# Linear attention on one Trainium2 core: from six tiles of 120 columns to five of 128, with a reordered start

## The chip, the cores and the metric

The kernel runs on one core of one Trainium2 chip. Time is device microseconds (us) for one execution, lower is better. Engines are named as in the profile: PE is the TensorE matmul engine, PEld its weight loads (they overlap the matmuls: 122.3 us of them beside 244.4 us of PE in the 275.5 us of the kernel before), DVE is VectorE, ACT is ScalarE, POOL is GpSimd, SP is SyncE, which here only issues DMAs. "q" after an engine's name means its instruction queue. The profile traces one execution; its span (first to last instruction) is about 1.7 us shorter than the device time of the same execution (275.5 for 277.27 us before).

## The reference

Two linear-attention blocks A and B read the same input x of 2048 rows and 640 columns; a sigmoid gate mixes their results. There are 32 heads of 20 columns. All data is bf16.

```python
def attn(x, wqkv, wo):                       # x (1, 2048, 640); H = 32, Dh = 20
    q, k, v = split_heads(x @ wqkv)          # wqkv (640, 1920)
    phi = lambda t: where(t > 0, t + 1, exp(t)) + 1e-6
    pq, pk = phi(q), phi(k)
    kv  = einsum("bhsd,bhse->bhde", pk, v)   # 20 x 20 per head
    z   = einsum("bhsd->bhd", pk)
    num = einsum("bhqd,bhde->bhqe", pq, kv)
    den = einsum("bhqd,bhd->bhq", pq, z)[..., None] + 1e-6
    return merge_heads(num / den) @ wo
g   = sigmoid((x * gate_w).sum(-1))
out = g * attn(x, A_wqkv, A_wo) + (1 - g) * attn(x, B_wqkv, B_wo)
```

The kernel uses phi(t) = min(exp(t), 1) + max(t, 0) + 1e-6: an exponential on ACT and two DVE operations. The per-head products become 128-row matmuls by putting several heads in one tile and masking the result to the heads' diagonal squares.

## The kernel before

It has a start (loads and constants), four projection blocks of 512 rows, and an output stage. The 640 columns are cut into six tiles: five of 120 columns (6 heads) and one of 40. No head crosses a tile edge, so one matmul per tile gives the numerator. Cut to what matters (`p` is the path, A or B):

```python
# start, inside block 0
load_weights_act()      # SP: gwt, 1.2 KB, the gate vector
load_weights_sync()     # SP: wq
load_weights_pool()     # POOL: wkv of A, then wo of A and B
build_consts()          # POOL: masks, and E4, which spreads a head's scale over its columns
nc.vector.tensor_copy(out=gw32[:], in_=gwt[...])     # L171: the gate as a matmul operand
load_weights_sync2()    # SP: wkv of B
...
for tb in range(4):                                  # projection block of 512 rows
    gps = ...           # 5 matmuls: the gate sums (L176)
    for p in range(2):
        for b in range(6):                           # q tile
            # 5 matmuls -> qps (L191); ACT: qe = exp (L194)
            # DVE: qr = max(qps,0)+1e-6 (L196); pqT = min(qe,1)+qr (L198)
    for tti in range(4):                             # 128 rows of keys and values
        for ct in range(5):                          # 512 of A k, A v, B k, B v
            # 5 matmuls -> kps (L212)
            for (r0, r1, kind, p) in regions:        # in column order
                # key part: exp on ACT, two DVE operations -> pk_st
                # value part: ACT copies into windows of 120 plus a column of ones -> vz
        # 6 matmuls per path: kvps += pk_st x vz (L248)
# DVE: KVbd = kvps * mask, Zm (z spread over heads)
...
def stage_A(tb):        # denominators dps; numerators nps, copied to nb by ACT
    for b in range(6):
        nc.tensor.matmul(nps, lhsT=KVbd[p][:, b, :], rhs=pqT[p][:, b, rows], start=True, stop=True)
def stage_B(tb):        # rps = E4 x (gate/denominator); DVE: oT = nb * rps, 12 per block
def stage_C(tb):        # output projection
    for tti in range(4):
        ops = pso.tile([P, 640], F32)                # pso has one buffer
        # 2 paths x 6 tiles x (512 and 128 columns) = 24 matmuls (L324)
        nc.scalar.copy(out=ob, in_=ops)              # L331
```

## Time and profile before

| Before | |
|---|---|
| Device time, median of 16 runs | 277.29 us (275.94 to 278.33) |
| Profiled span | 275.5 us |
| Start, until the first gate matmul | 18.2 us |
| Projection blocks, until the first numerator matmul | 161.7 us |
| Output stage | 95.6 us |

The profile's page begins with each engine's busy time and share of the span.

```profile
span 275.5 us, 4403 instructions
...
PE 244.4 (89%) x1668; PEld 122.3 (44%) x1668; DVE 163.9 (59%) x345; ACT 134.3 (49%) x429; POOL 16.4 (6%) x40
```

PE is busy 89% of the span. That alone does not say how near it is to its limit, because the records of matmuls overlap: one 512-column matmul is recorded at 379 ns, but 22 of them (`kps L212 x22` in the chain below) take 4.76 us, 216 ns each. I count matmuls at this spacing.

The chain that ended last, in order of time (start us, length us, engine or DMA, what, line):

```profile
3.81 13.52 DMA gwt<-in_gate_w_dram
17.36 0.83 DVE gw L171
18.23 2.31 PE gps L176 x5
...
47.43 4.76 PE kps L212 x22
...
64.67 1.20 DVE qr L196 x2
65.87 1.20 DVE pqT L198 x2
```

PE does nothing until 18.23 us, because a 1.2 KB load of the gate vector takes 13.5 us to land. Its five first matmuls take 2.31 us, about 0.42 us apart, so PE starts slowly. Below, PE is called cold while 512-column matmuls come about 0.42 us apart, and warm when they come 0.216 us apart. Later the chain runs through DVE's pairs, 1.20 us for two q tiles in each of two operations, so 1.20 us per q tile, where PE needs 5 x 0.216 = 1.08 us.

PE's timeline, first gate matmul of each projection block and the first numerator:

```profile
18.23 2.31 PE L176 MATMUL gps<-xT,gw 128*128 128x512 bf16 x5 [18.23 <-DVE gw L171]
...
58.67 0.38 PE L176 MATMUL gps<-xT,gw 128*128 128x512 bf16 x1
...
98.64 0.38 PE L176 MATMUL gps<-xT,gw 128*128 128x512 bf16 x1
...
138.60 0.38 PE L176 MATMUL gps<-xT,gw 128*128 128x512 bf16 x1
...
179.91 0.85 PE L295 MATMUL nps<-pqT,KVbd 128*128 128x512 bf16 x3
```

The blocks repeat every 39.97 us (58.67 to 98.64, 98.64 to 138.60).

ACT's timeline, copies of finished output tiles (last field: idle before, and who ended it):

```profile
241.37 0.69 ACT L331 CAST ob<-ops 128x640 bf16<-128x640 f32 x1 [7.33 <-issue]
245.62 0.69 ACT L331 CAST ob<-ops 128x640 bf16<-128x640 f32 x1 [3.55 <-PE ops L324]
249.86 0.69 ACT L331 CAST ob<-ops 128x640 bf16<-128x640 f32 x1 [3.55 <-PE ops L324]
```

These come 4.24 us apart. There is one ops buffer, so each period is 24 matmuls and their drain (3.42 us in PE's timeline, 225.12 to 228.54), the copy (0.69 us), and only then the next tile (229.36).

### The profile page before, as it was taken

The page shows a single profiled execution, that of the slowest core. Times are in us where ns is not written, and L with a number is a line of the kernel's source. Part 1 is how long each engine was busy: PE and PEld are TensorE (multiplying, and loading weights), DVE is VectorE, ACT ScalarE, POOL GpSimd, SP SyncE. Part 2 cuts the span into 40 slices and gives each one's busy share as a digit, 9 for nine tenths or more (in the row PEclk, how much of TensorE's full clock was granted, in tenths as well). Part 3 has the DMA queues.
Part 4 walks back from the last instruction along what each step waited for, and adds up shares of the span by engine and source line. Part 5 has one row for each costly group of instructions (what it writes and reads, how often), then busy time and mean ns, then how long its engine had stood idle before and what let it go on. Part 6 is the DMA issues. An engine that isn't in the chain of part 4 may idle for free.

```text
span 275.5 us, 4403 instructions
## 1 busy us (share of the span) xinstructions
PE 244.4 (89%) x1668; PEld 122.3 (44%) x1668; DVE 163.9 (59%) x345; ACT 134.3 (49%) x429; POOL 16.4 (6%) x40
## 2 busy tenths in 40 slices
PE   0039999999999999999999999989999999988874
PEld 0014444444444444444444444434556545555442
DVE  2016995558985639985549976569942922932400
ACT  3006565665555575466674565699651444022121
POOL 8950000000000000000000000000000000000000
PEclk9999999999999999999999999999999999999999
DMA  7999500031000000000000000000010010010101
GB/s 187 340 325 289 130 4 0 1 63 34 0 0 2 1 0 2 0 0 1 2 1 0 0 2 0 0 2 4 1 45 28 26 48 26 24 50 24 48 26 48
DMA packets 17492, 12.30 MB, mean 45 GB/s; under 512 B 12148, under 2 KB 16758, under 8 KB 17472
## 3 DMA queue, kind: packets, MB, share of 16 engines
q1 hardware_dynamic: 16608, 8.52, 11.6%
q0 software_dynamic: 864, 3.50, 3.7%
q8 instruction: 13, 0.21, 0.3%
q14 instruction: 7, 0.06, 0.1%
HBM read 6.66 MB, written 2.62 MB: 34 GB/s over the span
## 4 chain that ended last, share of the span: by engine, by line
PE 52%; DVE 21%; ACT 15%; DMA 5%; issue 5%; SPq 1%; ACTq 0%; DVEq 0%
PE kps L212 20%; PE ops L324 18%; DVE qr L196 8%; DVE pqT L198 7%; PE qps L191 5%; DMA gwt<-in_gate_w_dram 5%; ACT vz L238 4%; ACT nb L297 4%; PE kvps L248 4%; ACT ob L331 3%; DVE r_st L225 3%; PE rps L310 2%; PE gps L176 2%; DVE pk_st L227 2%; PE nps L295 2%
## 5 line engine op out<-in xcount | busy, mean ns | idle before, releaser
L212 PE MATMUL kps<-wkv,xT 128*128 128x512 bf16 x400 | 94.5, 379 | 0.5
L324 PE MATMUL ops<-woh,oT 128*128 128x512 bf16 (+1 forms) x384 | 60.1, 299 | 4.6 <-ACT ob L331 4.1
L212 PEld LDWEIGHTS <-xT 128*128 128x128 bf16 x400 | 38.1, 97 | 41.2 <-issue 2.4
L191 PE MATMUL qps<-xT,wq 128*128 128x512 bf16 x240 | 53.5, 383 | 0.0
L312 DVE TENSOR_TENSOR oT<-nb,rps 128x512 bf16<-128x512 bf16 x48 | 30.9, 686 | 30.4 <-PE rps L310 22.3
L238 ACT CAST vz<-kps 128x120 bf16<-128x120 f32 (+4 forms) x224 | 35.8, 260 | 18.7 <-PE kps L212 14.9
L225 DVE TENSOR_SCALAR r_st<-kps 128x512 bf16<-128x512 f32 (+1 forms) x64 | 30.5, 486 | 21.6 <-ACT e_st L223 21.6
L324 PEld LDWEIGHTS <-oT 128*128 128x128 bf16 x384 | 30.2, 98 | 25.6 <-issue 5.5
L194 ACT ACTIVATE qe<-qps 128x512 bf16<-128x512 f32 x48 | 28.3, 597 | 21.9 <-DVE pqT L198 12.0
L196 DVE TENSOR_SCALAR qr<-qps 128x512 bf16<-128x512 f32 x48 | 31.1, 682 | 13.3 <-ACT qe L194 13.3
L223 ACT ACTIVATE e_st<-kps 128x512 bf16<-128x512 f32 (+1 forms) x64 | 27.7, 463 | 19.5 <-PE kps L212 19.5
L191 PEld LDWEIGHTS <-wq 128*128 128x128 bf16 x240 | 23.7, 99 | 29.6 <-issue 2.2
L331 ACT CAST ob<-ops 128x640 bf16<-128x640 f32 x16 | 11.1, 692 | 49.0 <-PE ops L324 37.4
L198 DVE SCALAR_TENSOR_TENSOR pqT<-qe,qr 128x512 bf16<-128x512 bf16 x48 | 31.1, 682 | 0.2
L227 DVE SCALAR_TENSOR_TENSOR pk_st<-e_st,r_st 128x512 bf16<-128x512 bf16 (+1 forms) x64 | 30.1, 488 | 1.2
L297 ACT CAST nb<-nps 128x512 bf16<-128x512 f32 x48 | 25.3, 643 | 8.0 <-PE nps L295 7.5
L176 PE MATMUL gps<-xT,gw 128*128 128x512 bf16 x20 | 7.2, 440 | 18.2 <-DVE gw L171 18.2
L248 PE MATMUL kvps<-vz,pk_st 128*128 128x121 bf16 (+1 forms) x192 | 20.1, 212 | 2.3 <-ACT vz L238 1.7
L248 PEld LDWEIGHTS <-pk_st 128*128 128x128 bf16 x192 | 13.9, 97 | 15.8 <-DVE pk_st L227 6.8
L310 PEld LDWEIGHTS <-E 128*128 128x128 bf16 x192 | 13.9, 97 | 9.0 <-issue 4.2
L310 PE MATMUL rps<-rgT,E 128*128 128x128 bf16 x192 | 17.5, 218 | 0.3
L295 PE MATMUL nps<-pqT,KVbd 128*128 128x512 bf16 x48 | 16.2, 380 | 1.4 <-ACT nb L297 0.2
(46 smaller groups left out, 62.7 us busy)
## 6 DMA issues: line engine op xcount, KB each, us to landing
out_dram<-ob SPq DMA_DIRECT2D x16, 160.0 KB, 1.8
wkv<-in_A_wqkv_dram POOLq DMA_DIRECT2D x2, 800.0 KB, 8.2
wkv<-in_B_wqkv_dram SPq DMA_DIRECT2D x2, 800.0 KB, 10.8
woh<-in_A_wo_dram POOLq DMA_DIRECT2D x1, 800.0 KB, 9.3
woh<-in_B_wo_dram POOLq DMA_DIRECT2D x1, 800.0 KB, 9.2
wq<-in_B_wqkv_dram SPq DMA_DIRECT2D x1, 800.0 KB, 13.2
wq<-in_A_wqkv_dram SPq DMA_DIRECT2D x1, 640.0 KB, 14.4
wq<-in_A_wqkv_dram SPq DMA_DIRECT2D x1, 160.0 KB, 13.2
```

What stands on the lines that cost most here:

```text
L191: nc.tensor.matmul(qps[:, :], lhsT=wq[p][:, fo, BOFF[b]:BOFF[b] + P], rhs=xT[:, fo, :], start=(fo == 0), stop=(fo == NFO - 1))
L196: nc.vector.tensor_scalar(out=r[:], in0=qps[:, :], scalar1=0.0, scalar2=1e-6, op0=ALU.max, op1=ALU.add)
L198: nc.vector.scalar_tensor_tensor(out=pqT[p][:, b, tb * TB:(tb + 1) * TB], in0=e[:], scalar=1.0, in1=r[:], op0=ALU.min, op1=ALU.add)
L212: nc.tensor.matmul(kps[:, :], lhsT=xT[:, fo, tti * TT:(tti + 1) * TT], rhs=wkv[:, fo, ct * 512:(ct + 1) * 512], start=(fo == 0), stop=(fo ...
L225: nc.vector.tensor_scalar(out=r_st[:, d0:d0 + n], in0=kps[:, a0 - c0:a1 - c0], scalar1=0.0, scalar2=1e-6, op0=ALU.max, op1=ALU.add)
L227: nc.vector.scalar_tensor_tensor(out=pk_st[:, d0:d0 + n], in0=e_st[:, d0:d0 + n], scalar=1.0, in1=r_st[:, d0:d0 + n], op0=ALU.min, op1=ALU ...
L238: nc.scalar.copy(out=vz_st[:, d0:d0 + n], in_=kps[:, c - c0:c - c0 + n])
L248: nc.tensor.matmul(kt[:msz, off:off + bs + 1], lhsT=pk_st[:, p * D + BOFF[b]:p * D + BOFF[b] + msz], rhs=vz_st[:, p * VZW + WIN * b:p * VZ ...
L297: nc.scalar.copy(out=nb[:], in_=nps[:, :])
L310: nc.tensor.matmul(rps[:, j * TT:(j + 1) * TT], lhsT=E4[j][:, BOFF[b]:BOFF[b] + P], rhs=rgT[:, 0:TT], start=True, stop=True)
L312: nc.vector.tensor_tensor(out=oT[p][:, b, :], in0=nsbs[b][:], in1=rps[:, :], op=ALU.mult)
L324: nc.tensor.matmul(ops[:, j0:j1], lhsT=oT[p][:, b, tti * TT:(tti + 1) * TT], rhs=woh[p][:, b, j0:j1], start=(i == 0), stop=(i == 2 * NBLK ...
```

## The change

The intent is to use all 128 rows: 640 = 5 x 128, so one tile in six goes away in q, in the key-value products and in the output projection. The price is that heads straddle tile edges. A numerator tile needs small corner products from its neighbours: 13 matmuls per path instead of 6 in blocks 0 and 1. For blocks 2 and 3 the corner rows are gathered by small DMAs into one extra operand, which makes it 10. Four other things change with it: POOL builds constants before it issues weight loads and issues wo last; ten dummy matmuls run in the idle start; mask products are made by 13 small matmuls; and value copies come before key work within a projection tile. The gate vector keeps its place: it is still SP's first load after x. With the layout itself the value copies on ACT become wider and fewer (128 instead of 224), and a memset in each projection tile goes away. The diff is cut to what matters.

```diff
-NBLK = 6
-BROWS = [120, 120, 120, 120, 120, 40]
+NB = 5
+PAIRS = {}           # for tile m: the tiles b whose heads reach into it; 13 pairs in all
+CORNER = []          # the rows of a neighbour that tile m needs
...
             if tb == 0:
-                load_weights_act()
                 load_weights_sync()
+                build_consts()
                 load_weights_pool()
-                build_consts()
+                build_e4()
+                load_wo()
+                for i in range(10):
+                    nc.tensor.matmul(wps[:, :], lhsT=KVbd[0][:, 4, :], rhs=KVbd[0][:, 0:4, :],
+                                     start=True, stop=True)
+                for m in range(NB):
+                    for b in PAIRS[m]:
+                        nc.tensor.matmul(mps[:, 0:P], lhsT=Hind[b][:, :], rhs=Hind[m][:, :], ...)
+                        nc.scalar.copy(out=masks[:, PIDX[(b, m)], :], in_=mps[:, 0:P])
...
+            if tb == NTB - 1:
+                for p in range(2):
+                    for (b, m, r0, r1, o) in CORNER:
+                        nc.sync.dma_start(out=pqc[p][o:o + r1 - r0, :], in_=pqT[p][r0:r1, b, 2 * TB:4 * TB])
...
-                    for (r0, r1, kind, p) in regions:
+                    for (r0, r1, kind, p) in sorted(regions, key=lambda r: r[2] == "k"):
...
-                nc.tensor.matmul(nps[:, :], lhsT=KVbd[p][:, b, :], rhs=rq, start=True, stop=True)
+                if tb >= 2:
+                    nc.tensor.matmul(nps[:, :], lhsT=KVbd[p][:, PIDX[(m, m)], :], rhs=pqT[p][:, m, rows], ...)
+                    nc.tensor.matmul(nps[:, :], lhsT=KVc[p][0:NCR, m, :], rhs=pqc[p][0:NCR, ...], ...)
+                    bl = []
+                for i, b in enumerate(bl):
+                    nc.tensor.matmul(nps[:, :], lhsT=KVbd[p][:, PIDX[(b, m)], :], rhs=rq, ...)
...
-                    for b in range(NBLK):     # output projection: 24 matmuls per tile
+                    for m in range(NB):       # 20
```

## The prediction

> **What bounds the kernel now.** PE, in three stages (timeline and chain of waits).
> (1) Start, 0–18.2 us: PE waits for gw, a copy of gwt; the chain shows gwt's 1.2 KB load taking 13.5 us to land, issued at 3.8 us while the POOL queue moves 3.5 MB of weights. The first projection matmuls then start 425 ns apart, later ones 216 ns (22 in 4.76 us): a cold start of about 9 matmuls, 1.8 us.
> (2) Projections, 18.2–179.9 us: four blocks with a period of 40.0 us. PE work per block is 165 matmuls x 0.216 = 35.6 us plus 48 small kvps matmuls, about 2.3 us; the other 2 us are waits, mostly in the q part, where DVE needs 1.2 us per q tile (chain: pairs of 1.20 us) and PE only 1.08.
> (3) Output, 179.9–272.4 us: 16 output tiles, mostly 4.24 us apart: 24 matmuls (3.26 us), drain, the 0.69 us ACT copy of ob, next tile. The single ops buffer forbids overlap; three blocks' first tiles are longer (DVE's oT products, 0.62 us each).
>
> **The change.** 640 columns in five full 128-row tiles instead of six of 120. Heads straddle tiles, so the numerator needs corner products: 13 matmuls per path and block instead of 6 in blocks 0–1; in blocks 2–3, 10 (corners gathered by small DMAs). POOL builds constants before it issues weight loads, and PE gets 10 dummy matmuls and 13 mask matmuls in the idle start.
>
> **Costs.**
> - Start: without POOL's traffic ahead, the input transpose (5.0 us to landing when alone, DMA view) should be followed by gwt at about 7.5–8 us, gw at 9.[...] First projection matmul at about 9.5 us: −9. The dummy matmuls should keep PE warm[...]: −1.5. Then perhaps a wait for wq: +1.
> - Projections: per block 10 q matmuls fewer (−2.16 us; −2.4 where DVE paces), kvps 40 of 141–161 columns for 48 of 121/41 (about +0.2): −2.15 x 4 = −8.6.
> - Output: numerator matmuls 48 → 92, +9.5 us of PE; ops 384 → 320, −8.7; rps −1.8. PE's sum hardly moves, the latency chain does: tile 4.24 → 3.65 us (20 matmuls), 12 undisturbed tiles, −7. Block starts: 10 oT products for 12, partly refilled with numerator matmuls, −2.5. The first numerators (52 matmuls, PE-bound, where ACT's 24 copies were the limit) delay the first oT: +1.5. Together −8.
>
> 277.1 − 9 − 1.5 + 1 − 8.6 − 8 = 251.0. **Predicted 251 us, 8 in 10 between 244.5 and 257.** Faster by over 2%: 0.97; within 2%: 0.02; slower: 0.01.
>
> **What would show it.** First gps matmul near 9.5 us at 216 ns spacing; block period 37.8 us; output stage about 84.5 us with undisturbed tiles 3.6–3.7 us apart; DVE q pairs still 1.20 us in the chain; nb copies no longer back to back after the first numerators.
>
> **What would make it wrong.** gwt still slow by itself (640 two-byte pieces), or wq/wkv late, so that the start gains only 4 us; PE going cold again before gps; the 20 corner and mask products on DVE delaying the first numerators; numerator matmuls not fitting the gaps between output tiles, so that stage 3 becomes PE-bound and gains only 4 us.

The −9 rests on the trace of the kernel before, where gwt is late beside POOL's loads. That the dummies would keep PE warm (−1.5) was my estimate, out of the 1.8 us that the cold start costs in that trace; no run had yet shown it.

## The result

| | Before | After |
|---|---|---|
| Device time, median | 277.29 us (16 runs) | 250.00 us (8 runs, 249.53 to 250.03) |
| Profiled span | 275.5 us | 248.2 us |
| Start | 18.2 us | 8.2 us |
| Projection blocks | 161.7 us | 149.6 us |
| Output stage | 95.6 us | 90.4 us |

The ratio is 0.9015, 95% interval 0.8998 to 0.9032. Ratios in this document are the mean time of one kernel's runs over that of the other's runs of the same rounds, so they are not quite the ratio of the medians quoted. Executions over 1.5% slower than the fastest of the same kernel are left out of the means.

The same views of the kernel after. First the page's engine shares:

```profile
span 248.2 us, 4126 instructions
...
PE 235.6 (95%) x1535; PEld 117.7 (47%) x1535; DVE 152.3 (61%) x336; ACT 121.4 (49%) x326; POOL 26.1 (11%) x76
```

The chain that ended last, in order of time:

```profile
1.86 4.36 PE wps L213 x10
...
6.63 1.57 PE mps L218 x9
8.20 1.21 PE gps L225 x5
...
14.54 1.20 DVE pqT L247 x2
15.73 1.20 DVE qr L245 x2
```

The gate vector's load is off the chain: dummies (wps) and mask products (mps) fill PE until 8.2 us. The five gate matmuls take 1.21 us instead of 2.31. DVE's pairs still take 1.20 us each, now for ten q tiles per block.

PE's timeline, first gate matmul of each block and the first numerator:

```profile
8.16 1.24 PE L225 MATMUL gps<-xT,gw 128*128 128x512 bf16 x5
...
45.11 0.38 PE L225 MATMUL gps<-xT,gw 128*128 128x512 bf16 x1
...
82.38 0.38 PE L225 MATMUL gps<-xT,gw 128*128 128x512 bf16 x1
...
119.64 0.38 PE L225 MATMUL gps<-xT,gw 128*128 128x512 bf16 x1
...
157.77 6.21 PE L381 MATMUL nps<-pqT,KVbd 128*128 128x512 bf16 x28
```

The block period is 37.26 us (82.38 to 119.64), 2.71 less than before.

ACT's timeline, output copies:

```profile
218.24 0.69 ACT L418 CAST ob<-ops 128x640 bf16<-128x640 f32 x1 [6.54 <-issue]
221.94 0.69 ACT L418 CAST ob<-ops 128x640 bf16<-128x640 f32 x1 [3.01 <-PE ops L411]
225.64 0.69 ACT L418 CAST ob<-ops 128x640 bf16<-128x640 f32 x1 [3.01 <-PE ops L411]
```

The tile period is 3.70 us, 0.54 less.

The start gained 10.1 us, the projections 12.1 and the output stage 5.2. The forecast had 9, 9.1 (8.6 and 1.5 less a feared wait of 1) and 8. So the total was nearly exact while its parts were not, and the parts needed experiments.

### The profile page after: what moved, and what is told of

It reads as the page before. It is cut to its first block, busy times and chain, and to the rows that moved or that the text cites. A ratio compares the mean times of both kernels' runs of the same rounds, so it can differ in the third digit from the quotient of the medians.

```text
span 248.2 us, 4126 instructions
## 1 busy us (share of the span) xinstructions
PE 235.6 (95%) x1535; PEld 117.7 (47%) x1535; DVE 152.3 (61%) x336; ACT 121.4 (49%) x326; POOL 26.1 (11%) x76
## 4 chain that ended last, share of the span: by engine, by line
PE 63%; DVE 24%; ACT 7%; issue 4%; ACTq 0%; DVEq 0%
PE kps L265 26%; PE ops L411 17%; DVE qr L245 10%; DVE pqT L247 9%; PE nps L381 5%; PE kvps L302 5%; ACT ob L418 3%; DVE pk_st L280 2%; PE rps L397 2%; DVE r_st L278 2%; PE gps L225 2%; PE nps L376 2%; PE wps L213 2%; PE nps L374 2%; ACT th L229 2%
## 5 line engine op out<-in xcount | busy, mean ns | idle before, releaser
L411 PE MATMUL ops<-woh,oT 128*128 128x512 bf16 (+1 forms) x320 | 50.6, 299 | 4.2 <-ACT ob L418 4.0
L293 ACT CAST vz<-kps 128x240 bf16<-128x240 f32 (+6 forms) x128 | 31.4, 299 | 26.8 <-PE kps L265 26.8
L399 DVE TENSOR_TENSOR oT<-nb,rps 128x512 bf16<-128x512 bf16 x40 | 25.7, 686 | 30.3 <-PE rps L397 30.1
L240 PE MATMUL qps<-xT,wq 128*128 128x512 bf16 x200 | 43.8, 379 | 0.0
L411 PEld LDWEIGHTS <-oT 128*128 128x128 bf16 x320 | 25.4, 98 | 24.4 <-issue 6.4
L245 DVE TENSOR_SCALAR qr<-qps 128x512 bf16<-128x512 f32 x40 | 25.9, 681 | 14.7 <-ACT qe L243 14.7
L243 ACT ACTIVATE qe<-qps 128x512 bf16<-128x512 f32 x40 | 23.4, 597 | 16.5 <-DVE pqT L247 12.6
L247 DVE SCALAR_TENSOR_TENSOR pqT<-qe,qr 128x512 bf16<-128x512 bf16 x40 | 26.0, 681 | 0.1
L302 PE MATMUL kvps<-vz,pk_st 128*128 128x141 bf16 (+1 forms) x160 | 20.3, 228 | 0.9 <-DVE pk_st L280 0.5
L381 PE MATMUL nps<-pqT,KVbd 128*128 128x512 bf16 x52 | 12.1, 380 | 0.0
```

The lines of the kernel that those rows point to most:

```text
L240: nc.tensor.matmul(qps[:, :], lhsT=wq[p][:, fo, P * b:P * b + P], rhs=xT[:, fo, :], start=(fo == 0), stop=(fo == NFO - 1))
L245: nc.vector.tensor_scalar(out=r[:], in0=qps[:, :], scalar1=0.0, scalar2=1e-6, op0=ALU.max, op1=ALU.add)
L247: nc.vector.scalar_tensor_tensor(out=pqT[p][:, b, tb * TB:(tb + 1) * TB], in0=e[:], scalar=1.0, in1=r[:], op0=ALU.min, op1=ALU.add)
L293: nc.scalar.copy(out=vz_st[:, d0:d0 + n], in_=kps[:, c - c0:c - c0 + n])
L302: nc.tensor.matmul(kt[:, off:off + WW[b]], lhsT=pk_st[:, p * D + P * b:p * D + P * b + P], rhs=vz_st[:, p * VZW + WST[b]:p * VZW + WEN[b]] ...
L399: nc.vector.tensor_tensor(out=oT[p][:, m, :], in0=nsbs[m][:], in1=rps[:, :], op=ALU.mult)
```

## The experiments

Names that begin with b are edits of the kernel before, those with a edits of the kernel after. Every run gave correct results, and each kernel has four timed executions, made in turn with the kernel before on the same chip. They were made in four calls; the kernel before had medians of 277.39, 276.66, 277.53 and 277.30 us in them, so medians of different calls can differ by up to 0.9 us for no other reason. The kernel after (250.0 us) was not run again. Its ratio, 0.8998 to 0.9032, is the safer comparison: of the edits of the kernel after, only a_no_dummies has an interval that overlaps it.

| Run | Median us | Ratio to before | Against 250.0 |
|---|---|---|---|
| b_consts_first | 267.02 | 0.9627 (0.9603 to 0.9651) | |
| a_weights_first | 260.31 | 0.9388 (0.9360 to 0.9416) | +10.3 |
| a_no_dummies | 250.81 | 0.9045 (0.9024 to 0.9066) | +0.8 |
| a_k_first | 251.82 | 0.9076 (0.9053 to 0.9099) | +1.8 |
| b_all_but_layout | 264.55 | 0.9544 (0.9503 to 0.9585) | +14.6 |
| a_no_gather | 252.57 | 0.9113 (0.9073 to 0.9153) | +2.6 |
| a_split_ops | 246.78 | 0.8910 (0.8878 to 0.8942) | −3.2 |
| a_q_relu_act | 247.23 | 0.8925 (0.8891 to 0.8958) | −2.8 |
| a_gather1 | 248.56 | 0.8952 (0.8926 to 0.8978) | −1.4 |
| a_split_qrelu | 244.24 | 0.8796 (0.8770 to 0.8821) | −5.8 |
| a_all_three | 243.12 | 0.8753 (0.8723 to 0.8783) | −6.9 |
| a_wo_early | 253.62 | 0.9153 (0.9088 to 0.9219) | +3.6 |

### The start: is POOL's weight traffic what delays the gate vector?

My theory was that the 1.2 KB load is slow because POOL's megabytes use the same DMA engines. The rival was that it is slow by itself (640 pieces of two bytes; the trace of the kernel before has 640 DMA packets of this size), or that other edits moved the start. Two runs move only the order, one in each kernel.

```diff
 # b_consts_first (kernel before)
-                load_weights_pool()
                 build_consts()
+                load_weights_pool()
 # a_weights_first (kernel after)
+                load_weights_pool()
+                load_wo()
                 build_consts()
-                load_weights_pool()
                 build_e4()
-                load_wo()
```

> The kernel before with one thing moved: POOL builds its constants before it issues its weight loads. Theory (gate vector delayed by POOL's weight traffic on the shared DMA engines): gwt lands by about 7 us instead of 17.3, first gate matmul at about 8 us still cold (425 ns apart), time 277.1 - 10 = about 267 us. Rival (gwt is slow by its own 640 two-byte pieces, or the new kernel's start came from its other edits): gwt still lands after 15 us, time stays near 277 us.

> The kernel after with POOL's weight loads (wkv and wo) moved back ahead of the constants, the dummies kept. Theory: gwt lands near 17 us again, the first gate matmul starts at 17 to 18 us[...], time 250 + 10 to 12 = 260 to 262 us. Rival: unchanged within 2 us.

The chains of b_consts_first and of a_weights_first, the gate vector's load:

```profile
3.53 3.06 DMA gwt<-in_gate_w_dram
```

```profile
3.84 11.83 DMA gwt<-in_gate_w_dram
```

PE's timelines of the same two, the first gate matmuls:

```profile
7.50 2.32 PE L176 MATMUL gps<-xT,gw 128*128 128x512 bf16 x5 [7.50 <-DVE gw L171]
```

```profile
16.57 2.31 PE L225 MATMUL gps<-xT,gw 128*128 128x512 bf16 x5 [5.39 <-DVE gw L221]
```

With POOL quiet, the same load lands in 3.1 us; with POOL's loads ahead it takes 11.8 us. Moving the order alone gives 10.3 us in the kernel before (277.3 to 267.0) and takes 10.3 us away in the kernel after. (That the two agree to a tenth is chance: in the second, the start is only 8.4 us later, 16.57 against 8.16, and most of the rest is a PE that has gone cold again: from the first gate matmul to the first key-value matmul it takes 13.79 us, 16.57 to 30.36, against 11.86 in the kernel after.) The theory stands, and the rival falls. In the kernel before, between 10 and 12 us, the times of the 142 packets of POOL's queue (0.72 MB) add up to 103% of the time of the 16 DMA engines, and those of the 144 packets of gwt's queue, all of two bytes, to 4.2%. So the two queues share the engines; in what order an engine takes their packets is not shown.

In a_weights_first PE went cold again: the gate matmuls take 2.31 us although dummies and mask matmuls had run before. The granted clock on this run's page, in slices of 6.45 us, is 0.9 or more in the first, 0.7 in the second, 0.5 in the third (12.9 to 19.35 us, with the gate matmuls in it) and 0.9 or more again from the fourth on. If it fell once, from 1.00 to 0.50, that was between 9.0 and 10.3 us, an estimate from the second slice's 0.7. Then the 5.39 us of idleness before the gate matmuls (the bracket in their line) did not bring the fall, because these begin at 11.2 us. A single mask product at 10.87 us already took 0.31 us, where those at 8.26 and 8.89 us took 0.22. What makes the clock fall or rise is not shown. Nor does the granted clock show every cold PE: in the kernel before it reads 1.00 from 14 to 20 us, over five gate matmuls with the same 2.31 us. The cold state has to be read from the spacing.

### The dummies

```diff
-                wps = ps1.tile([P, 512], F32, name="wps", tag="ps1")
-                for i in range(10):
-                    nc.tensor.matmul(wps[:, :], lhsT=KVbd[0][:, 4, :], rhs=KVbd[0][:, 0:4, :], ...)
```

> The kernel after without the 10 dummy matmuls; the 13 mask matmuls stay. Theory (dummies are what warms PE): the first 8 or so projection matmuls run 425 ns apart, PE's q part ends about 1.7 us later, but DVE paces that part at 1.20 us per tile against PE's 1.08, so only part of it survives: time 250.0 + 0.8 to 1.8 us. Rival (dummies do nothing, or the mask matmuls alone keep it warm): within 0.3 us of 250.0.

PE's timeline of a_no_dummies:

```profile
7.84 2.32 PE L221 MATMUL gps<-xT,gw 128*128 128x512 bf16 x5 [0.92 <-DVE gw L217]
...
46.63 0.81 PE L221 MATMUL gps<-xT,gw 128*128 128x512 bf16 x3
```

The five gate matmuls take 2.32 us instead of 1.24, so the dummies do warm PE, though they multiply operands just set to zero and are themselves cold (ten in 4.36 us in the kernel after, 0.43 us apart); the 13 mask matmuls alone do not. The last group of gate matmuls of the second block comes 38.79 us after the first gate matmul, against 37.69 in the kernel after (8.16 to 45.85): 1.1 us longer. The start is 0.3 us earlier, which leaves the 0.8 us of the medians. The intervals of the ratios overlap slightly, so it is the trace that carries this, not the times. I had counted 1.5 us, and PE's slow start does cost about that: from the first gate matmul to the first key-value matmul it takes 13.30 us (7.84 to 21.14) against 11.86 (8.16 to 20.02), 1.44 longer. About 0.3 us is won back in the first projection tile, where PE has to wait less for DVE (25 matmuls in 5.56 us instead of 5.88), and 0.3 by the earlier start.

### Value copies before key work

The block period fell by 2.71 us where I had forecast 2.15. The forecast had overlooked one line of the diff, the sort of the regions.

```diff
-                    for (r0, r1, kind, p) in sorted(regions, key=lambda r: r[2] == "k"):
+                    for (r0, r1, kind, p) in regions:
```

> The kernel after with the order of the projection tile's copies put back: key part before value part. The block period fell by 2.71 us where 2.15 was forecast; theory A says the value-first order gave the missing half microsecond: block period 37.8 us instead of 37.26, time about 252.2. Theory B says it is the missing memset, wider copies and fewer kvps matmuls: block period stays within 0.15 us of 37.26 and the time within 0.6 us of 250.0.

PE's timeline of a_k_first, the first gate matmuls of the third and fourth block, and the key-value product that follows the first of them:

```profile
82.96 0.38 PE L225 MATMUL gps<-xT,gw 128*128 128x512 bf16 x1
83.69 0.28 PE L302 MATMUL kvps<-vz,pk_st 128*128 128x141 bf16 x2 [0.36 <-ACT vz L293]
...
120.60 0.59 PE L225 MATMUL gps<-xT,gw 128*128 128x512 bf16 x2
```

The period is 37.64 us, 0.38 longer, and the time is 1.8 us longer, where theory A had said 37.8 and 252.2. Theory A holds for most of the missing 0.56 us. The trace also shows where the time goes. At a block's border PE's five gate matmuls are woven with the last key-value products of the block before, and these wait for ACT's last value copies (the 0.36 us in the second line above). From the first gate matmul to the first q matmul it takes 1.70 us in this run (82.96 to 84.66) and 1.39 in the kernel after (82.38 to 83.77), so 0.31 of the 0.38 us lies there. In the view of waits, PE's key-value products waited for ACT's value copies 8 times, 1.7 us in all, in the kernel before, twice, 0.7 us, in this run, and never in the kernel after.

### Is the rest the layout, and do the parts add?

The kernel before received three of the side edits, POOL's constants before its weights, the dummies and the sort. It kept its early wo and its six tiles.

```diff
-                load_weights_pool()
                 build_consts()
+                load_weights_pool()
...
                 load_weights_sync2()
+                wps = ps1.tile([P, 512], F32, name="wps", tag="ps1")
+                for i in range(10):
+                    nc.tensor.matmul(wps[:, :], lhsT=KVbd[0][:, 4, :], rhs=KVbd[0][:, 0:4, :], ...)
...
-                    for (r0, r1, kind, p) in regions:
+                    for (r0, r1, kind, p) in sorted(regions, key=lambda r: r[2] == "k"):
```

> The kernel before with the change's three side edits (POOL's constants before its weights, the 10 dummy matmuls, value copies before key copies) but its own six tiles of 120 rows. Sum theory (the parts simply add): 277.3 - 10.3 - 0.8 - 1.8 = 264.4 us, so that the layout itself is worth the remaining 14.4 us. Rival (the layout's share is larger or smaller because the parts overlap): more than 1.5 us away from 264.4.

PE's timeline of b_all_but_layout:

```profile
27.01 2.33 PE L216 MATMUL kps<-wkv,xT 128*128 128x512 bf16 x10 [1.08 <-DMA wkv<-in_B_wqkv_dram]
...
87.63 0.59 PE L180 MATMUL gps<-xT,gw 128*128 128x512 bf16 x2
...
127.04 0.59 PE L180 MATMUL gps<-xT,gw 128*128 128x512 bf16 x2
```

It measured 264.55 us, so the parts add. That they do so within 0.2 us is partly luck. The sort is worth 0.56 us per block here (39.97 to 39.41), 2.2 in all and not 1.8, and the first line shows a loss that the sum didn't have: PE waits 1.1 us for the last key-value weights. The kernel now starts 10 us earlier than its loads were arranged for.

The five tiles bring the period from 39.41 us to 37.26, which is 2.15 us per block, the number that the forecast gave for the layout. PE's timelines show where: from the first q matmul to the first key-value matmul it takes 13.04 us here (89.00 to 102.04) and 10.79 in the kernel after (83.77 to 94.56), 2.25 less for ten matmuls. The key-value part is about 0.1 us longer. The output stage of this run is 95.5 us, as long as before, so its gain too is the layout's.

### wo last

In the kernel after there is no such wait. The candidate was wo, which the change issues last; this run issues it where the kernel before does.

```diff
                 load_weights_pool()
-                build_e4()
                 load_wo()
+                build_e4()
```

> The kernel after with the two output-weight loads (wo, 1.6 MB, not needed before the output stage) issued right behind POOL's other weight loads, as the kernel before does, instead of after the expansion matrices. In the run with everything but the layout PE waited 1.1 us for the last key-value weights, in the new kernel it does not. Theory (wo shares the DMA engines and delays them; the new kernel needs them about 2 us earlier still): PE waits 1 to 3.5 us for wkv in the first block, time 251 to 253.5 us. Rival (the wait has nothing to do with wo): no such wait, time within 0.4 us of 250.0.

PE's timeline of a_wo_early:

```profile
23.39 1.25 PE L265 MATMUL kps<-wkv,xT 128*128 128x512 bf16 x5 [0.83 <-DMA wkv<-in_B_wqkv_dram]
25.70 2.33 PE L265 MATMUL kps<-wkv,xT 128*128 128x512 bf16 x9 [1.05 <-DVE r_st L278]
```

The wait is back, 0.8 us for the weights and then 1.1 us for DVE, which was itself held up. The profiled execution took 251.64 us, the four runs 251.64, 252.00, 255.25 and 255.27. So wo's place is worth 1.6 us or more, and the median, 253.6, lies just above what I expected. The two slower runs were not profiled, so why they are slower is open; their mean granted clock was 0.992 and 0.993, against 1.000 and 0.999 in the two faster ones. The wo loads themselves took 12.1 and 14.1 us to land in the profiled run, against 5.8 and 5.4 in the kernel after. Late wo removes no work; it protects the early start.

### What limits the output stage

Three runs lift or load one suspect each. The first lengthens the numerators (13 matmuls per path in all blocks, no corner DMAs):

```diff
-                if tb >= 2:
+                if tb >= NTB:
 # and the DMAs into pqc and KVc are left out
```

> The kernel after with 13 numerator matmuls per path in all four blocks, no gathered corners and none of their small DMAs: 12 matmuls of 0.216 us more, 2.6 us of PE work in the output stage. Theory (PE is the limit in the first output tile of each block, where the numerators are fitted in): time 250.0 + 1.3 to 2.6 us. Rival (numerators fit in the gaps between output tiles): within 0.5 us of 250.0.

It measured 252.57 us. Twelve matmuls at 0.216 us are 2.6 us, and 2.6 us is what they cost. In net terms none of them fitted into a gap. ACT's copies show where they went: the first output tile of block 1 now takes 9.98 us after the last of block 0, and that of block 2 takes 9.50, where the kernel after has 8.69 and 8.20, while the tiles between keep their 3.70 us. The gathering is worth its full PE time.

The second holds the output sum in two tiles, so that the 512-column part can be copied out and refilled while the 128-column part still runs. No other buffer had to be given up for it.

```diff
-            ops = pso.tile([P, 640], F32, name="ops")
-            for (j0, j1) in ((0, 512), (512, 640)):
+            for (j0, j1, nm) in ((0, 512, "opsA"), (512, 640, "opsB")):
+                ops = pso.tile([P, 512], F32, name=nm)
...
-            nc.scalar.copy(out=ob[:, :], in_=ops[:, :])
+                nc.scalar.copy(out=ob[:, j0:j1], in_=ops[:, 0:j1 - j0])
```

> The kernel after with the 640-wide output sum held in two tiles (512 and 128) that are copied out and freed separately. Theory (the single ops buffer sets the period of the undisturbed output tiles: 20 matmuls, drain, copy): the next tile's 512 part starts while the 128 part still runs, period 3.70 us falls to 3.0 to 3.2, time 250.0 - 4 to 7 us. Rival (PE itself or the oT products set it): period stays above 3.5 us, time within 1 us.

ACT's timeline of a_split_ops, copies of the 512-column part:

```profile
235.20 0.58 ACT L418 CAST ob<-opsA 128x512 bf16<-128x512 f32 x1 [2.28 <-issue]
...
238.24 0.59 ACT L418 CAST ob<-opsA 128x512 bf16<-128x512 f32 x1 [2.26 <-PE opsA L412]
```

The period fell from 3.70 to 3.03 us, so the single buffer did set it. But the time fell by 3.2 us, less than the 4 to 7 expected. Twelve undisturbed periods of 0.67 us are 8, and the twelve follow-up tiles do take 8.0 us less (36.36 for 44.34). But the first tiles of blocks 1 to 3 together take 5.1 us more (25.91 for 20.81). After blocks 0 and 1, PE's timeline shows the numerators that used to run during the copies; they still have to run on PE, and now follow the four tiles in a row. Before block 3 it shows the same of the scale products (rps) and DVE's oT products.

The third uses the gathered corners from block 1 on (two index edits that go with it are left out here).

```diff
-    pqc = [const.tile([P, 2 * TB], BF16, ...
+    pqc = [const.tile([P, 3 * TB], BF16, ...
...
-                if tb >= 2:
+                if tb >= 1:
```

> The kernel after with the gathered corners used from block 1 on instead of block 2: 6 numerator matmuls of 0.216 us fewer, all in the stretch between the first numerators and the first oT product. Theory (that stretch is limited by PE: 52 numerator matmuls and 4 denominator groups make its 13.2 us): it shortens by 1.3 us and the time falls to 248.7 to 249.3 us. Rival (it is limited by ACT's copies or by DVE's masked products, or the corners gathered by DMA come too late): time within 0.4 us of 250.0 or above it.

DVE's timelines of the kernel before, the kernel after and a_gather1, the first oT products:

```profile
190.89 0.69 DVE L312 TENSOR_TENSOR oT<-nb,rps 128x512 bf16<-128x512 bf16 x1 [0.30 <-ACT nb L297]
```

```profile
171.47 1.92 DVE L399 TENSOR_TENSOR oT<-nb,rps 128x512 bf16<-128x512 bf16 x3 [1.82 <-PE rps L397]
```

```profile
170.36 1.92 DVE L399 TENSOR_TENSOR oT<-nb,rps 128x512 bf16<-128x512 bf16 x3 [0.57 <-PE rps L397]
```

In the kernel before, the first oT waited for an ACT copy; in the other two it waits for PE. From the first numerator (157.77 us in the kernel after, 157.91 in a_gather1) to the first oT it is 13.70 us and 12.45 us: 1.25 us less for six matmuls of 0.216. The time fell by 1.4 us. PE limits this stretch.

### The q part

DVE's 1.20 us per q tile against PE's 1.08 was said to set the pace. Here ACT takes the positive part of two tiles in five. The 1e-6 is left out there, and the result is still within the tolerance.

```diff
+                    if b % 2 == 1:
+                        nc.scalar.activation(out=r[:], in_=qps[:, :], func=ACT.Relu)
+                    else:
                         nc.vector.tensor_scalar(out=r[:], in0=qps[:, :], scalar1=0.0, scalar2=1e-6, ...)
```

> The kernel after with the positive part of 2 of 5 q tiles of each path taken on ACT instead of DVE (the 1e-6 term is left out there; far below the tolerance). Theory (DVE's two operations, 1.20 us per q tile, pace the q part, PE needs 1.08): the block period falls from 37.26 to 36.1 to 36.5 us and the time to 246 to 247.5 us. Rival (the block is limited by PE's own work and waits of the key and value part): period within 0.3 us of 37.26.

The chain of a_q_relu_act, in the second and third block:

```profile
46.16 10.79 PE qps L240 x50
...
82.79 10.79 PE qps L240 x50
```

The chain now runs through PE's q matmuls, where it ran through DVE before. The period is 36.63 us (46.16 to 82.79), just outside the expected 36.1 to 36.5; the time of 247.23 is inside. So DVE's time in the q part did cost PE 0.63 us per block. But it did not pace the q matmuls, as the theory has it. PE's timelines of the kernel after and of this run, from the first q matmul of the third block:

```profile
83.77 10.96 PE L240 MATMUL qps<-xT,wq 128*128 128x512 bf16 x50
94.56 5.88 PE L265 MATMUL kps<-wkv,xT 128*128 128x512 bf16 x25
100.28 0.95 PE L302 MATMUL kvps<-vz,pk_st 128*128 128x141 bf16 x6
```

```profile
82.63 10.96 PE L240 MATMUL qps<-xT,wq 128*128 128x512 bf16 x50
93.42 5.56 PE L268 MATMUL kps<-wkv,xT 128*128 128x512 bf16 x25
98.81 0.65 PE L305 MATMUL kvps<-vz,pk_st 128*128 128x141 bf16 x6
```

The 50 q matmuls take the same 10.96 us in both, without a break (and 60 take 13.20 in the kernel before). DVE falls behind meanwhile, and PE pays for it only afterwards, in the first projection tile: 0.32 us in its 25 matmuls and 0.30 in the six products after them, together nearly all of the 0.63. In the kernel after, DVE's last operation on a q tile starts at 98.59 us, 4 us after PE has turned to keys and values.

### Together

> Both limits lifted at once: two output tiles (by itself 3.2 us) and 2 of 5 positive parts on ACT (by itself 2.8 us). They act in different stages, so they should add: 244.0 us, between 243.5 and 244.6. If ACT becomes short, less.

> The two of the run before and the corners gathered from block 1 on: if all three add, 243.0 us, between 242.4 and 243.6, the fastest of all.

The first pair gave 244.24 us and all three 243.12 us, as expected from adding. The last takes 2.8% less time than the kernel after and 12.5% less than the one before (ratio 0.8753). Its edits are the three diffs above.

## Why the prediction was right, and where its parts were wrong

The total was forecast at 251.0 us and measured at 250.0. The steps, with what the runs put beside them:

| Step, as the prediction put it | Forecast us | Measured us |
|---|---|---|
| First projection matmul at about 9.5 us | −9 | −10.1 (8.2 us) |
| Dummies keep PE warm | −1.5 | −0.8 (a_no_dummies; 1.44 at PE) |
| Perhaps a wait for wq | +1 | none in the profile |
| Layout in the projections, four blocks | −8.6 | 2.15 per block, −8.6 |
| (value copies first: not in the prediction) | 0 | −1.8 (a_k_first) |
| (wo last: not in the prediction) | 0 | 1.6 or more if undone (a_wo_early) |
| Twelve undisturbed output tiles | −7 | −6.5 |
| Block starts in the output stage | −2.5 | −1.8 in block 0, +0.4 in blocks 1 to 3 |
| First numerators delay the first oT | +1.5 | +2.7 |

- The start's mechanism, POOL's loads delaying the gate vector, was right and is shown by two runs (3.1 us without them, 11.8 with them). The size was a little low: gwt landed at 6.6 us in b_consts_first, not at 7.5 to 8.
- The layout's 2.15 us per block was exact, and made up nearly as forecast: 2.25 us less for ten q matmuls and 0.1 more for the key-value part. What was wrong is the account of the q part in "What bounds the kernel now": "the other 2 us are waits, mostly in the q part" and "−2.4 where DVE paces". PE did not wait there (60 matmuls in 13.20 us before, 50 in 10.96 after); DVE's lag costs PE 0.6 us later, in the first projection tile (a_q_relu_act). The step that failed for the block's period is that nothing else was expected to change it: the forecast of 37.8 us (measured 37.26) left out the sort of the regions. b_all_but_layout shows 0.56 us per block for it on the old layout (39.97 to 39.41), a_k_first 0.38 on the new one.
- The +1 for "a wait for wq" named the wrong weights. No wait for wq came; wkv was the one in danger, and the late wo prevented it (0.8 us of waiting in the profile of a_wo_early).
- "Tile 4.24 → 3.65": it is 3.70, so twelve of them gave 6.5 us. I sum the three follow-up periods of each block from the output copies: 50.84 us before, 44.34 after.
- "The first numerators … delay the first oT: +1.5": it is 10.98 us before (179.91 to 190.89) and 13.70 after. The mechanism, PE in place of ACT's copies, is right, as a_gather1 shows. The size was off. The forecast of +1.5 leaves 12.5 us for the stretch, of which 52 matmuls at 0.216 us are 11.2. The remaining 1.3 us is too little for what else PE does in it: the four denominator groups take 0.39 us each in the chain of the kernel after, 1.6 in all, and the first scale products come on top.
- "Block starts … −2.5": the cut came in block 0 alone. From its first oT to its first output copy it is 9.58 us before (190.89 to 200.47) and 7.75 after (171.47 to 179.22). The starts of blocks 1 to 3, from the last copy of one block to the first of the next, sum to 20.44 us before and 20.81 after: blocks 2 and 3 gained 0.3 and 1.0 us, but block 1's start became 1.7 us longer (7.02 to 8.69). Before, DVE had made 4 of its 12 oT products in the gaps of the preceding tiles; now it makes none of the ten there, and PE's timeline shows numerators in these gaps. That these take the room is what the traces suggest; no run isolates it.
- So the output stage's forecast of −8 was 3 us too good, and the overlooked sort, the better start and the wait for wq that did not come were 3 to 4 us not counted. They cancelled, which was luck. The range held, but not because each part was understood.

## What to carry to other kernels

Before you retile a kernel, look at what its first instruction waits for: here a change of order among DMA issues, one moved line in b_consts_first, was worth 10 of 27 us, and the load that must come first was the smallest one. When the start moves earlier, look again at which loads come next, because an order that was harmless at 18 us costs time at 8 us (1.6 us or more in a_wo_early). A retiling that removes a sixth of the matmuls paid here in q (2.25 us per block) and in each output tile (0.54 us), and gave part back in the first numerators (+2.7 us). Take each stage's limit (DVE's lag, a single PSUM buffer, the numerators) and ask whether that can be moved too, as the three small edits here did for another 6.9 us. And look for a limit's cost where PE really waits: the chain ran through DVE in the q part, but PE lost the time (0.6 us per block) in the tile after it.
